# A convolution mixed with linear attention: the written-out order, the engines of the read-outs and the PSUM rings replaced by new tables

## The chip, the cores and the metric

The kernel runs on one core of a Trainium2 chip. Its engines work side by side, each through its own list of instructions in order: TensorE (PE in the profile; its weight loads are PEld), VectorE (DVE), ScalarE (ACT), GpSimd (POOL) and SyncE (SP), which issues most of the DMAs. An engine waits for another one through semaphores. The metric is the device time of one execution in microseconds; lower is better. The profile's span runs from the first to the last instruction of the program, a little less than the execution.

## The reference

Two branches share one input `x` of 2048 rows and 512 channels. Branch a is a long convolution along the rows, with one kernel for each channel that is a sum of 128 complex exponentials (written as an FFT in the reference). Branch b is a linear attention with 32 heads of 16, whose features are softmax pairs of a small learned projection. A sigmoid gate mixes them row by row.

```python
x = A_u
g = _sigmoid((x * gate_w).sum(-1, keepdims=True))
# a: K[d,l] = Re sum_n C[d,n] * exp(l*dt[d]*A[d,n]) * dt[d]*B[d,n];  y = irfft(rfft(u)*rfft(K))[:L] + u*Dskip
P = jnp.exp(logdA[:, :, None] * l[None, None, :])
K = jnp.einsum("dn,dnl,dn->dl", Cc, P, dB).real
# b: per head
phi_q = jnp.concatenate([_softmax(pq, axis=-1), _softmax(-pq, axis=-1)], axis=-1)
phi_k = jnp.concatenate([_softmax(pk, axis=-1), _softmax(-pk, axis=-1)], axis=-1)
num = jnp.einsum("bhqf,bhfd->bhqd", phi_q, kv)
den = jnp.einsum("bhqf,bhf->bhq", phi_q, z)[..., None] + 1e-6
b = (num / den) @ wo
return g * a + (1 - g) * b
```

## The kernel before

The program is a list of about a thousand steps, built by `Plan.add` and `Plan.dma`, each with its engine, its inputs and the rings of buffers that it takes and frees. `Plan.run` doesn't search for an order. It reads three tables of digits: `ORDER` names the steps in the order in which their instructions are written out, `SIDES` says of every step that may run on either of two engines which one it gets (0 or 1 of its pair; mostly copies out of PSUM, the read-outs, on ScalarE or VectorE), and `RINGS` says which of two PSUM rings a step takes its banks from. Each engine then executes its own instructions in that order. So the place of a step in `ORDER` fixes what stands ahead of it on its engine, on SyncE's queue of DMAs too.

The work falls into four stretches.

First come the loads, sine tables for the transforms (`tgs`), transposes of `x` (`xps`) and the parameters of the exponentials.

Then come the keys of the attention in eight blocks. For each block TensorE makes two `pk` tiles, ScalarE takes Exp of plus and minus each (`ek`, tile Ek, L68), VectorE sums them to Zk (`zk`), ScalarE takes Ln of Zk and Exp of minus that (`rz`: the rows Zk<-Zk and vr<-Zk), and VectorE scales the values (`vr`). Between the blocks lie the transform of `x` (`XAu`, and `XU`, which reads the tile xst out) and the tables Ctab and Dtab of the convolution's kernel, whose sines and cosines ScalarE computes (`p_sn`, tile trg).

The third and longest stretch makes the convolution's kernel in sixteen units. For a unit ScalarE takes two sines (`cs<-args`) and one Exp (`E<-args`), VectorE makes the factors A (`A1`, L1132) and R (`Rh`, `Rl`), and TensorE multiplies them with 128 small matmuls (`kps`, L178). There is one buffer for A, so the next unit's `A1` waits for this unit's `kps`. Two units make a tile that goes through the transform (`psA`, `XA`, `psB`, `XK`), the product with the transform of `x` (`t`), the way back (`psz`, `Zr`, `psy`) and out. Beside it run the queries of the attention in four blocks (`eq`, tile Eq; `z1` to `z5`, tiles zs, den and apm: Ln and Exp again).

The last stretch finishes the last units and the output.

ScalarE evaluates Exp and Ln with one table of functions and Sin with another. Both are steps of `ORDER` like any other, five of each. No dependency ties a step that uses Exp to the table that is loaded when its turn comes; only the place in `ORDER` does. Where a function is called that the loaded table lacks, the build of the program puts a table load ahead of it, under the line of the call (L68). Copies, casts and Abs (L419) work with either table.

Of the kernel before, what the change touches and what calls it, by code (L numbers as in the profile page):

```python
# [70 lines left out]
class Plan:  # L71

    DIGITS = "0123456789abcdefghijklmnopqrstuvwxyzABCDEFGHIJKLMNOPQRSTUVWXYZ-_"
    ORDER = ("0H0I0J0M0K0W000L11122x0405060B0C0D2R0P0_100Q0d0e0f0X0N0S0y0z0A0s0t0u0U0708090V13140g0h0i0j0k0l2T2y0T0Y1716192S0O0102032U"
             "2V2W0Z1a0R1y0-2X1b2Z0m0n0o0a0b0c0p0q0r0v0w0x150E0F0G2_302-1c1n181w1z312Y1H1o2B1e1f1p1g1d1A32332C2D1x351I1J342L2E2J1C2K1B"
             "1q1r1s1E2F1K2H2M362G2P1F2N3738392I2Q2O3b3a4C1t1u1v4J4K4L4M4Y4Z4-4_3c4N1Y4Q4R4O3d3f4P3g4U4S4V50514W535758544T524X5b1P591D"
             "1M551O5d5c5e3h3e5i5m5j5f5g5n565a3i3j3k5h5o5k3l5q1h1i1j5s5r5t5x3n3m5B3o1Q5u5v1R5C5l5y5w5z5p3p3r5D5F5H5G5I5M5A3s5E5U3R2z3S"
             "3q3t3u3v5W5V5N2v2w1Z1G5J1L5X5K4D5L5_1S604E5O5Q5R5Y5Z5-5S61631T3w3y1N5P3x5T3z62671U693T4F3D6465684G6a3F1V666m3U6o3G6b6n6p"
             "1W3E3A3B3C6c3K3M6q3L3N3O3P3Q6d6r3V3W6s1X1-3X6e3Y3Z3H3I3J6f3_6g3-6h2040271_41422129222b23282d241k1l1m4344456t464748494b2a"
             "2f4a4c2c254d4e4f2e2g2h262o4g2j4i4j2i4n2k4h4k4l4m2l2q2s2p6i4o2r2m4p4q4r4s4t2t4u4w4v2n2u6u4x8l4y4z4A6j6k6x8p8k4B6l6v6w8m6y"  # L80
             "6z8o8q2A6A6B8n8r6G8s4H8t6F8w8u6I6J4I8x8z8y7M7N8Q8R8v8A6H8C6K6M8W8D8S8B6N8F7O9e9f9g6L7d8E9b9c9d8I6O8G7P7e8J7f8Z8H7Q6P7g8K"
             "8-6Q8X6R6S8L9h9i9j6T7h7i8T938U8_an8M8V7jao948Nae8O7k8P6U6V6W6X6Y6Z6_70717R8Yaf90ap7l7m9192a4a8956C6D6Ea9ag6-a69673a5abah"
             "75a7akaaac747Sadai7n977o99alaj7298atam9a7p7q7r7s7t767u7v7w7y7z7AaBaCaq77au7Tar799n7U9oaHas9v9p787V7Wav9w9x7aaw9qaE9raK7X"
             "7YaL7Z9y9z7-7_809DaDaM9EaI9L9M9A9B9CaxaFayc5c6bX7x7Caz7EaGb_aA9k9l9mc09FaJ7DbY7B7G7I7FaQ9N7bc1818283858687aNaR7JbZ7HaOaP"
             "aS84899s9t9ucba_b0b1aYaZa-c7c8c2888a9GaTb-9HaU7c8b8d8fc9c3aVaW8ccPcQcRceca7K8gaXcc8e8hc4cf7Lcg9I9J9K9O8ib88j9P9Q9R9Scdcs"
             "ckchb9bgba9T9U9VcictbhclcjdYd-cBbicudZcmbocycvd_e0cCbwcnb2b3b4bpcDbxcwe1cocqczcrcxbbbje2bce3cpb5b6b7cHe4bqeUeVe59W9X9Ybd"
             "bebfcAcIbkcEdOeL9ZeMeWcFdP9-dSdTcGbye6e7e8cJblbmbna0cScTcU9_a1cKeOeRa2cLcYcZc-e9eaebdUedeeefbrcMeNa3bscNcOePbzbAc_d7eSdR"
             "e-eQecd0bBbCbDeTd1d8dfbtbubvdWcVcWcXdgegeXd2ehbEbFbGd3d9dnd4d5d6eidodQeYdae_dVeZdbdhbHbIbJfpf0dpfsftdXfqfvfrdcdddedidjbK"
             "dqbLezeAeBf1drfKbMfLf2f3dkdldmf4fwf5bNfubOfMfxfQfyf6f7fzdsdtdufNbPfAfOfReFeGeHdBfPf8bQfBfCejekfDfbfSdvdwdxdydzdAdCdEfTfc"
             "fUfVdDeCeDeEfddFf9eIeJeKfWfXfYdGdHfZfaf-fef_fffEg0elbRbSbTfFfgfGfHembUbVbWepeqerdIdJdKesg1endLdMdNeoewexeyfhg2fifmfnfofj"  # L90
             "fkfleteuevfIg3g4g5g6fJg7gbgcgdg8g9ga")
    SIDES = ("111101000110111000001000111100100110111000001100100000000001000111101010110100001000000100000001000000000000000100000000"
             "01000000000000000111000110000100000001000001100100010")
    RINGS = ("100111001111001000100000000000000000000001100000000000000001100010000000100100010000011111110110111101000010000011101010"
             "0110")
    WARM = ("000000000000000000000000000000000000000000000000000000000000000000000000000000000000000000000000000000000000000000000000"
            "000000000000000000000")
    ZPS = ("01000111")
# [49 lines left out]
    def run(self):  # L148
        code = {d: i for i, d in enumerate(self.DIGITS)}
        order = [64 * code[a] + code[b] for a, b in zip(self.ORDER[0::2], self.ORDER[1::2])] or list(range(len(self.nodes)))  # L150
        assert sorted(order) == list(range(len(self.nodes)))
        sides, rings, warm = iter(self.SIDES), iter(self.RINGS), iter(self.WARM)
        for n in self.nodes:
# [1496 lines left out]
```

## Time and profile before

| | |
|---|---|
| time, median of 3 runs | 267.77 us (266.85 to 270.31) |
| the profiled execution | 266.68 us, span 264.9 us |
| mean granted TensorE clock | 0.939 |
| VectorE busy | 225.0 us (85% of the span) |
| ScalarE busy | 220.3 us (83%) |
| TensorE matmuls busy | 198.5 us (75%), 4642 matmuls and as many weight loads |
| bytes moved by DMA | 34.63 MB |

VectorE and ScalarE are busy almost alike, and for most of the time both at once, so that neither has much room alone. TensorE's busy time is that of short, pipelined matmuls. In a row of a group of instructions the number behind x is a count, then come the busy time in us, the mean of one in ns, and the idle time of the engine just before such instructions with what ended it; "issue" stands for idle time in which the profile shows nothing that the engine waited for.

### The profile page before, as it was taken

To read this page: it belongs to the slowest core of one execution; us is meant where nothing else is said; L and a number is where in the kernel's file an instruction comes from. 1 tells how busy PE (TensorE), PEld (TensorE's weight loads), DVE (VectorE), ACT (ScalarE), POOL (GpSimd) and SP (SyncE) were. 2 spreads that over 40 slices of the span, in tenths; PEclk is the share of its full clock that TensorE was granted. 3 is DMA by queue.
4 is the path that set the end of the run, shared out by engine and by line. 5 is a ranking of instruction groups with operands and counts; after the bars stand their busy time and mean duration, and the time that the engine had idled before them with its cause. 6 is when DMAs were issued, how large, how long until landed. Compare 5 with 4: busy or idle time off the path is not lost.

```text
span 264.9 us, 10337 instructions
## 1 busy us (share of the span) xinstructions
PE 198.5 (75%) x4642; PEld 134.3 (51%) x4642; DVE 225.0 (85%) x297; ACT 220.3 (83%) x305; POOL 20.6 (8%) x36
## 2 busy tenths in 40 slices
PE   0478999999955653999566867479968888986980
PEld 0377565566634321344434635357637565875540
DVE  7698989998899999899679998667998998965771
ACT  6896878999999783999899999679998999852550
POOL 4770000000000000000000000000000000020331
PEclk9999999999997575799988999999999999999996
DMA  7899300043270743700530358921596789897316
GB/s 197 147 208 190 76 2 4 2 121 108 90 194 12 235 123 109 227 28 4 155 109 2 109 127 217 301 50 23 117 245 153 211 207 233 218 224 246 62 37 105
DMA packets 54252, 34.63 MB, mean 131 GB/s; under 512 B 34400, under 2 KB 49920, under 8 KB 53824
## 3 DMA queue, kind: packets, MB, share of 16 engines
q1 hardware_dynamic: 53664, 32.73, 49.0%
q0 software_dynamic: 544, 1.25, 2.2%
q8 instruction: 36, 0.59, 1.0%
q14 instruction: 8, 0.07, 0.1%
HBM read 21.38 MB, written 12.58 MB: 128 GB/s over the span
## 4 chain that ended last, share of the span: by engine, by line
PE 38%; ACT 31%; DVE 16%; issue 7%; SPq 3%; DMA 3%; ACTq 0%; POOLq 0%; POOL 0%; DVEq 0%
PE pk L738 5%; ACT cs L68 5%; ACT Eq L68 4%; PE vp L786 4%; PE kps L178 3%; PE psy L853 3%; PE psz L1284 3%; ACT E L68 3%; ACT XA L144 3%; DVE Ctab L393 2%; DVE Dtab L393 2%; ACT XK L144 2%; DMA XUX<-XUd 2%; ACT L65 2%; ACT Zr L144 2%
## 5 line engine op out<-in xcount | busy, mean ns | idle before, releaser
L68 ACT ACTIVATE cs<-args 128x1024 bf16<-128x1024 f32 x32 | 31.0, 1046 | 6.2 <-PE args L1055 6.2
L1132 DVE TENSOR_TENSOR A<-Ctab,Dtab 128x3072 bf16<-128x3072 bf16 x16 | 28.1, 1756 | 9.5 <-PE kps L178 9.4
L178 PE MATMUL kps<-R,A 128*32 128x64 bf16 x2048 | 21.6, 198 | 11.9 <-issue 7.8
L178 PEld LDWEIGHTS <-A 128*32 128x32 bf16 x2048 | 19.8, 116 | 15.5 <-issue 13.2
L1399 POOL DMA_DIRECT2D out_dram<-xT x10 | 6.5, 652 | 229.3 <-ACT Ctab L144 217.1
L1141 DVE TENSOR_TENSOR R<-E,cs 128x2048 bf16<-128x2048 bf16 x16 | 19.5, 1218 | 0.5 <-ACT E L68 0.5
L1145 DVE TENSOR_TENSOR R<-E,cs 128x2048 bf16<-128x2048 bf16 x16 | 19.5, 1218 | 0.1
L144 ACT CAST XA<-psA 128x1024 bf16<-128x1024 f32 (+1 forms) x15 | 14.5, 983 | 5.2 <-PE psA L185 5.1
L1256 DVE TENSOR_TENSOR t<-XUX,XK 128x2048 bf16<-128x2048 bf16 x14 | 17.0, 1219 | 2.0 <-DMA XUX<-XUd 1.2
L1284 PE MATMUL psz<-t,TI 128*128 128x512 bf16 x64 | 16.8, 380 | 2.3 <-issue 0.8
L144 ACT CAST XK<-psB 128x1024 bf16<-128x1024 f32 (+1 forms) x16 | 15.9, 1023 | 3.0 <-PE psB L191 2.5
L68 ACT ACTIVATE E<-args 128x1024 bf16<-128x1024 f32 x16 | 17.0, 1061 | 0.9 <-PE args L1077 0.9
L786 PE MATMUL vp<-WW,xT 128*128 128x512 bf16 x64 | 17.6, 410 | 0.0
L68 ACT ACTIVATE Ek<-pk 128x512 bf16<-128x512 f32 x32 | 16.5, 606 | 1.2 <-PE pk L738 1.2
L872 PE MATMUL pq<-xT,Wqp 128*128 128x512 bf16 x64 | 16.9, 401 | 0.4 <-ACT Eq L68 0.4
L68 ACT ACTIVATE Eq<-pq 128x512 bf16<-128x512 f32 (+1 forms) x28 | 16.8, 726 | 0.3 <-PE pq L872 0.3
L144 ACT CAST Zr<-psz 128x1024 bf16<-128x1024 f32 (+1 forms) x15 | 14.7, 986 | 2.5 <-PE psz L1284 2.3
L645 PE MATMUL psB<-XAu,TB 64*128 64x128 bf16 x256 | 10.7, 240 | 7.4 <-ACT xst L144 6.2
L738 PE MATMUL pk<-WW,xT 128*128 128x512 bf16 x64 | 15.0, 380 | 0.0
L645 PEld LDWEIGHTS <-TB 64*128 64x128 bf16 x256 | 8.9, 105 | 10.3 <-issue 10.2
L185 PE MATMUL psA<-W,KD 128*64 128x128 bf16 x256 | 10.0, 221 | 4.6 <-ACT XK L144 1.4
L1055 PE MATMUL args<-selE,statC 64*128 64x512 bf16 x32 | 7.8, 463 | 7.2 <-DVE xst L146 3.7
(215 smaller groups left out, 511.5 us busy)
## 6 DMA issues: line engine op xcount, KB each, us to landing
XUX<-XUd SPq DMA_DIRECT2D x32, 256.0 KB, 4.7
XUd<-xst SPq DMA_DIRECT2D x8, 512.0 KB, 3.0
ax<-apd SPq DMA_DIRECT2D x16, 256.0 KB, 4.3
Zd<-Zr SPq DMA_DIRECT2D x12, 256.0 KB, 3.9
ZT<-Zd SPq DMA_DIRECT2D x12, 256.0 KB, 5.3
UD<-in_A_u_dram SPq DMA_DIRECT2D x16, 128.0 KB, 4.3
XUd<-xst SPq DMA_DIRECT2D x8, 256.0 KB, 4.0
Dtab<-in_B_wqkv_dram SPq DMA_DIRECT2D x1, 1024.0 KB, 5.8
```

The source lines that it names most:

```text
L68: return self.nc.scalar.activation(**kw)
L144: self.nc.scalar.copy(out=o, in_=i)
L178: nc.tensor.matmul(kps[32 * dj:32 * dj + 32, g4, e, :], lhsT=A[:, d // 4, 32 * ka:32 * ka + 32, d % 4], rhs=R[:, kr, d, :], start=(i == 0) ...
L645: nc.tensor.matmul(box.ps[:, c2, sl, :], lhsT=fc.TB[rows, b0:b0 + 2].rearrange("p a b -> p (a b)"), rhs=X.t[rows, k, r0 + sl].rearrange("p ...
L738: nc.tensor.matmul(box.ps[:], lhsT=xT[:, st, kt, :], rhs=g.WW[:, kt, :], start=(kt == 0), stop=(kt == 3))
L786: nc.tensor.matmul(box.ps[:], lhsT=xT[:, st, kt, :], rhs=g.WW[:, 4 + kt, :], start=(kt == 0), stop=(kt == 3))
L872: nc.tensor.matmul(box.ps[:, m - m0, :] if late else box.ps[:], lhsT=g.Wqp[:, kt, 128 * m:128 * m + 128], rhs=xT[:, 4 * b:4 * b + 4, kt, : ...
L1132: nc.vector.tensor_tensor(out=c.A[:].rearrange("p q (o a b) l -> p (q o) a b l", o=3, a=4), in0=cf.unsqueeze(2).to_broadcast([128, 96, 8, ...
L1141: nc.vector.tensor_tensor(out=c.R[:, :, :, 32:64], in0=t.E[:, 1].unsqueeze(1).to_broadcast([128, 2, 32, 32]), in1=t.cs[:], op=ALU.mult)
L1145: nc.vector.tensor_tensor(out=c.R[:, :, :, 0:32], in0=t.E[:, 0].unsqueeze(1).to_broadcast([128, 2, 32, 32]), in1=t.cs[:, ::-1, :, ::-1], o ...
L1256: nc.vector.tensor_tensor(out=box.t, in0=Ls[r0 // ns].X[:], in1=box.XK[:].unsqueeze(1).to_broadcast([128, 2, 1024]), op=ALU.mult)
L1284: nc.tensor.matmul(box.pz[:, hb, :], lhsT=fc.TIp[:, k].rearrange("p h a t -> p (h a t)"), rhs=box.t[:, k, 512 * hb:512 * hb + 512], start= ...
```

## The change

Three tables get new values: `ORDER`, `SIDES` and `RINGS`. The steps, their instructions, their shapes and the numbers of buffers stay as they are; `WARM` and `ZPS` are not touched. Two lines of the diff stand for all:

```diff
-    ORDER = ("0H0I0J0M0K0W000L11122x0405060B0C0D2R0P0_100Q0d0e0f0X0N0S0y0z0A0s0t0u0U0708090V13140g0h0i0j0k0l2T2y0T0Y1716192S0O0102032U"
...
+    ORDER = ("070B0H0I0y0C0d000K0J0L0g0M0D0S0p0W0z150j0U110q0_2R010N0a040V0A0e0P142x2S0Q2T192U0X100r0T0m0h050O2y2V0s0R0k0n0Y2X0Z170l0-"
...
-    SIDES = ("111101000110111000001000111100100110111000001100100000000001000111101010110100001000000100000001000000000000000100000000"
...
+    SIDES = ("111101010111110100000000011101101000000000000100000000000000110101001010111110101100100100011100000000000100000000100010"
```

In `SIDES`, 23 steps go from ScalarE to VectorE and 20 the other way, six of them `XU` (tile xst). In `RINGS` 39 of the steps that may use either of two rings take the other one.

On ScalarE, among the blocks of the keys, before (Dtab is made by Exp; vb and xst are read-outs):

```order
L68 ACTIVATE Ek<-pk 128x512 x4
L144 CAST XAu<-psA 128x256x4
L68 ACTIVATE Dtab<-pt_223 128x128x4 x2
L144 CAST vb<-vp 128x512
L68 ACTIVATE Zk<-Zk 128x128
L68 ACTIVATE vr<-Zk 128x4x32
L68 ACTIVATE Ek<-pk 128x512 x4
L144 CAST xst<-psB 128x2x4x4x32
```

and at the same stage now (trg is a sine):

```order
L65 ACT_TABLE_LOAD
L144 CAST XAu<-psA 128x256x4
L68 ACTIVATE trg<-pb_220 128x1024
L68 ACTIVATE trg<-pb_219 128x1024
L144 CAST vb<-vp 128x512
L68 ACT_TABLE_LOAD
L68 ACTIVATE Zk<-Zk 128x128
L68 ACT_TABLE_LOAD
L68 ACTIVATE vr<-Zk 128x4x32
L144 CAST xst<-psB 128x2x4x4x32
L68 ACTIVATE Ek<-pk 128x512 x4
```

Before, all eight blocks' Ek, Zk and vr stand ahead of the change to the sine table; now that change (`tabT`, the row L65) stands after the second block's Ek, the sines trg stand between the later blocks, and each return from a sine to Ln and Exp has table loads under L68.

On ScalarE, at the second query block, before (cs is a pair of sines; zs and den are Ln and Exp):

```order
L68 ACTIVATE zs<-zs 128x256
L68 ACTIVATE den<-zs 128x256
L65 ACT_TABLE_LOAD
L68 ACTIVATE cs<-args 128x1024 x2
L144 CAST KD<-kps 128x1024
L68 ACTIVATE cs<-args 128x1024 x6
L144 CAST wo<-ops 128x512
L65 ACT_TABLE_LOAD
```

and now:

```order
L65 ACT_TABLE_LOAD
L68 ACTIVATE cs<-args 128x1024 x2
L68 ACT_TABLE_LOAD
L68 ACTIVATE zs<-zs 128x256
L68 ACT_TABLE_LOAD
L68 ACTIVATE den<-zs 128x256
L68 ACTIVATE Eq<-pq 128x4x128 x2
L68 ACTIVATE E<-args 128x1024
L68 ACTIVATE Eq<-pq 128x4x128 x2
L68 ACT_TABLE_LOAD
L68 ACTIVATE den<-den,eps 128x128
L68 ACT_TABLE_LOAD
```

The eight sines of four units stood together between two loads; now Ln and Exp stand between them, with a load at each turn. Over the whole program ScalarE's list has 11 rows ACT_TABLE_LOAD before (one L233, ten L65) and 53 now (one L233, ten L65, 42 L68). Of the 42, 25 stand between the early L65 load shown above and the last Eq of the first query block, and 17 between that and the last pair of sines; none stands after it. One of the ten L65 loads now stands at the end of ScalarE's list, with nothing behind it.

On VectorE, around the change from Ctab0 to Ctab1 (the eighth to the ninth A, which waits for the eighth unit's `kps`), before:

```order
L1132 TENSOR_TENSOR A<-Ctab_74,Dtab 128x3072
L1145 TENSOR_TENSOR R<-E,cs 128x64x32
L943 TENSOR_TENSOR Eq<-Eq,ax 128x2048
L1141 TENSOR_TENSOR R<-E,cs 128x64x32
L1085 TENSOR_TENSOR E<-E,Gtab 128x1024
L1132 TENSOR_TENSOR A<-Ctab_75,Dtab 128x3072
```

and now:

```order
L1132 TENSOR_TENSOR A<-Ctab_74,Dtab 128x3072
L146 CAST xT<-bps 128x4x128
L1141 TENSOR_TENSOR R<-E,cs 128x64x32
L943 TENSOR_TENSOR Eq<-Eq,ax 128x2048
L146 CAST Dtab<-ops 128x512
L943 TENSOR_TENSOR Eq<-Eq,ax 128x2048
L1085 TENSOR_TENSOR E<-E,Gtab 128x1024
L146 CAST Dtab<-ops 128x512
L1145 TENSOR_TENSOR R<-E,cs 128x64x32
L1132 TENSOR_TENSOR A<-Ctab_75,Dtab 128x3072
```

Four other steps stood between the two A; now there are eight.

More of the change, by code (lines that the diff above doesn't have):

```diff
@@ L73 @@
     DIGITS = "0123456789abcdefghijklmnopqrstuvwxyzABCDEFGHIJKLMNOPQRSTUVWXYZ-_"
-    ORDER = ("0H0I0J0M0K0W000L11122x0405060B0C0D2R0P0_100Q0d0e0f0X0N0S0y0z0A0s0t0u0U0708090V13140g0h0i0j0k0l2T2y0T0Y1716192S0O0102032U"
[L75 to L91, printed above, removed]
@@ L92 @@
-    SIDES = ("111101000110111000001000111100100110111000001100100000000001000111101010110100001000000100000001000000000000000100000000"
-             "01000000000000000111000110000100000001000001100100010")
-    RINGS = ("100111001111001000100000000000000000000001100000000000000001100010000000100100010000011111110110111101000010000011101010"
-             "0110")
+    ORDER = ("070B0H0I0y0C0d000K0J0L0g0M0D0S0p0W0z150j0U110q0_2R010N0a040V0A0e0P142x2S0Q2T192U0X100r0T0m0h050O2y2V0s0R0k0n0Y2X0Z170l0-"
+             "0v1216022H060i2Y0w1d1a0f1b08130o2I0b1y2W1c1n0E0c1o1p2Z2_1e2-2F1H031I181f1w1z30310x0t1A331J352G1S360u091x1K1g321R2B1P2v1Y"
+             "1C2C1B371q2L1r342D1E2E2J1M2P1Z2M0F1h1F2N1L382K0G2Q393b1N1s2O4C4J4L1O3c3a3d4Y1Q3f1D4K1G4M1T4N3e4Z1U3h4Q3i4O1V1W3g4-3j4_3k"
+             "3l4P1X4R4U503n4V4W3m531i4S3o3p1_1-1j3r4T3R5154521t214X3q573s5b5c5d2758593w1k5i3y555e3t2856201u5f5j5a235m3z3u5g2a3x293S5q"
+             "5n4D5s5h3A4E3v1l5r2d3D3T3B5t2z5k3F5o5l3C3G5u223E1m5v3K5x3U3L3M5y2b5p5w3V3N2e243O3X5F5z2c5H3P3W3Z3H5G5I3-5B3I3Y3_5C2g5J5A"
+             "4F5M5D5K2540412f5E3Q2i43425Q445L453J5N465R2o472h5U5O5V5W482w5_492k4b1v5S5X604a2j5Y4c4d4g5Z2A5P4e4i2q5T5-4j63262l6467654f"
+             "696e4h612m2s2n62662p4n684p4k4l6a4q2r4m6f6m6b4o4u6n4w4x6c4v4r6i6d6o2t4y6j6g4s2u6t6p8n4t6k8k6x4z6y6h6q8r6u4A4B8t8o4G6r8u8C"
+             "8D8w8x8m6G6s6I8q6K8v8y8z6v6z8l6l4H6L6H8E8A6w6A4I6B6M6J8Q8R6N6F8B9e7d8p6O8S8F8s7M6P8G8I8J7f6Q7N8H9f8K7h9h9i8Z7e6R8W7g6S8L"
+             "7O8-6C8M8X6T8N7ian8T6U6V93ao7j8O6W7k8U8Pa48_7Q6D94a87la97mae7n9j8V6X7Paf7S8Y9091ap6Y6_927Ta5ak6Z7o9b6-95aa7096a6717397ah"
+             "6E7paiagab98a7aj759c9g99alac7q749aamat72auaB777r7R9daqaCar7s79ad9naDas7t9o9p7U9v7V7a7Wav9w9xaH7uaK7876aw7y9k7z9qaLaE7A7X"
+             "7v9r7Y9y9D7w9z9s9l7xaIaQ9A9E7Z7-9L9Max7C9mc5aybXc6aM9taF7B9F9Bazb_7baGaRb27Dc07EaA7_bY809Nc1aJ7FbZ81aYaN82859Ca_aO86837G"
+             "7I7caPaSc27HaTcb84b0aZ9GaU9H9u7J8789aV888ace9Ic7cf8b9O8daW9P8c8f7Ka-ccaXb88g8ec8cscgckb9clct7Lc99J8hb18i8jb-bgdY9Kcabhba"
+             "c39QcdchcydZbo9Rbicucicjbpd-bbcmd_cze0cvbccncw9SeUe1cBbwcCcPbxcx9TcDcob5eVb3cQcqcHcpe2cIb6bjb7cAcEcFcrbkc49WdOb4cGbqe3bd"
+             "9UbldSe4dT9Xbm9Z9YcJ9Ve5cKbyeObecSeLdPe6dUcYe79-a0cTeP9_cZa1bfe8cLcReMcMcNa2c-cObrbseQeRcUc_d0bneNe9eabzeSa3edbAd1d7eeeb"
+             "btbBd8bue-ezeAdfeffpbCdgbveTd9fqd2dneXeWe_cVcWeYd3bDdodaecdbd4dRcXeZegdQeBdhfrdWdpfKfLf0dcbEf1ehfsddd5d6ftbKeidedidVfvfw"
+             "dqdjbFejdrf2bGbHbIbJfuf4f3f5bLfxbMeCdkdlbNfQeDeEekfNfObOfMf6fPdsdtfRfyfzduf7dBbPf8dmfAeIfbfcfSfTdvfdfBeJdwdyeFbUeGdxdzeH"
+             "dAdCfUdEbQeKdDfVdFfCf9dGfDdHfEfafeelffdIfgbRfWfFfXdJemfGfYenfHfZeoepeqdLf_erbVg1f-esg0dKdMg3bWfhbSetdNfig2fIg4bTg5fJeuew"
+             "dXfjg6fkfmfnflg7gbgcfoexeyg8evg9gdga")
@@ L96 @@
+    SIDES = ("111101010111110100000000011101101000000000000100000000000000110101001010111110101100100100011100000000000100000000100010"
+             "11000000000000000011000000000100010001000000000011010")
+    RINGS = ("101000011101011100100000000000000000000000000000000000000001101001000000000000010111111001111011111010101101001001001111"
+             "0011")
     WARM = ("000000000000000000000000000000000000000000000000000000000000000000000000000000000000000000000000000000000000000000000000"
```

## The prediction

> **What bounds the kernel now.** I read the page's busy times and its chain first, then the windows of the four stretches that the words on the kernel tell of, then the waits and the timeline at the places where the new lists differ.
>
> ```profile
> PE 198.5 (75%) x4642; PEld 134.3 (51%) x4642; DVE 225.0 (85%) x297; ACT 220.3 (83%) x305; POOL 20.6 (8%) x36
> PE 38%; ACT 31%; DVE 16%; issue 7%; SPq 3%; DMA 3%; ACTq 0%; POOLq 0%; POOL 0%; DVEq 0%
> ```
>
> Three engines are used to three quarters and more, and the chain passes from one to the next. No single engine is the bound over the span; which one has least room differs by stretch:
>
> ```profile
> core 0: us, PE busy (x) PEld busy (x) DVE busy (x) ACT busy (x) POOL busy (x), PEclk, DMA share, GB/s
> 0.00:45.70 45.70, 32.35 (x371) 23.79 (x372) 39.40 (x78) 37.20 (x57) 12.99 (x24) 1.00 0.59 120
> 45.70:116.60 70.90, 54.77 (x1019) 31.96 (x1018) 66.41 (x98) 62.59 (x93) 0.00 (x0) 0.83 0.40 116
> 116.60:222.00 105.40, 79.67 (x2485) 54.82 (x2485) 90.68 (x92) 98.70 (x131) 0.00 (x0) 0.98 0.53 136
> 222.00:264.90 42.90, 31.70 (x793) 23.75 (x780) 28.53 (x32) 21.78 (x29) 7.57 (x12) 0.94 0.63 153
> ```
>
> I call these A (loads, tables), B (key blocks, up to the last Eq of the first query block), C (to the last pair of sines) and D (the rest). Each row gives the length, then the busy time of each engine. The idle time that ScalarE has left is 8.5 us in A, 8.3 in B, 6.7 in C and 21.1 in D. So whatever is added to ScalarE in B and C beyond 15.0 us must make these stretches longer. TensorE leaves 16.1 and 25.7 us there.
>
> **The change: table loads.** The order shows the largest piece: ScalarE's list has 53 table loads in place of 11. Their price and places before:
>
> ```profile
> L65 ACT ACT_TABLE_LOAD  x10: 1283/1283/1283, 2.2 to 223.0; - x10
> L233 ACT ACT_TABLE_LOAD x1 | 1.3, 1283 | 0.7 <-PEq L1634 0.7
> 0.00:45.70 45.70, 2.57 (x2) 1.00 0.59 120
> 45.70:116.60 70.90, 2.57 (x2) 0.83 0.40 116
> 116.60:222.00 105.40, 6.42 (x5) 0.98 0.53 136
> 222.00:264.90 42.90, 1.28 (x1) 0.94 0.63 153
> ```
>
> The first row gives the shortest, the median and the longest of ten loads, in ns: all alike. The four window rows count the loads of L65 by stretch. L233's lies in A, so before there are 3, 2, 5 and 1. By the new order there are 3, 26, 23 and 1, and the one in D stands last on ScalarE, where nobody waits for it. That is 24 more in B (24 x 1.283 = 30.8 us) and 18 more in C (23.1 us), 53.9 us in all.
>
> A load stands in ScalarE's own list, so what follows waits. It could cost more than its duration (a pause around it) or less (it runs while ScalarE waits for an operand). The timeline of ScalarE around one of them, and at two functions that follow each other without one (start, duration):
>
> ```profile
> 13.52 1.04 ACT L68 ACTIVATE TB<-tgv 128x1024 bf16<-128x1024 f32 x1
> 14.58 1.28 ACT L65 ACT_TABLE_LOAD   x1
> 15.87 0.63 ACT L68 ACTIVATE pt<-ld 128x512 f32<-128x512 bf16 x1
> 16.41 0.19 ACT L68 ACTIVATE dtc<-ldc 128x4 f32<-128x4 bf16 x1
> ...
> 70.38 0.31 ACT L68 ACTIVATE Zk<-Zk 128x128 f32<-128x128 f32 x1
> 70.73 0.31 ACT L68 ACTIVATE vr<-Zk 128x128 bf16<-128x128 f32 x1
> ```
>
> TB ends at 14.56, the load starts 0.02 later and ends at 15.86, and the next function starts 0.01 after it: no pause on either side. The two functions behind overlap by 0.09 (15.87 + 0.63 = 16.50 against 16.41). A load put between two that overlap costs this overlap too: 0.09 + 0.03 = 0.12 us each. Zk and vr, a Ln and an Exp of its result, don't overlap (70.69 against 70.73), so the loads inside such a pair (nine of the 42: seven in B, two in C) lose nothing. That leaves 18 x 0.12 = 2.2 us in B and 15 x 0.12 = 1.8 in C.
>
> The Trainium skill (ScalarE: Activation LUTs, What ACT_TABLE_LOAD costs) speaks harder against the change: a switch to another set is about 1283 ns of load and about 1380 ns of drain, 2.66 us together. The trace agrees with the first figure and shows nothing of the second (0.02 us ahead of the load at 14.58). By the page alone my estimate would be 58 us more.
>
> How much hides in idle time? ScalarE's two largest waits in B and C:
>
> ```profile
> ACT cs L68 <- PE args L1055: 5.1, 3, 4.2
> PE args L1055 <- DVE xst L146: 3.7, 1, 3.7
> ACT Dtab L144 <- PE ops L962: 2.6, 1, 2.6
> ```
>
> The first (us in all, times, longest) is in B: cs waits for args, and args for a read-out xst that stands late on VectorE. All six xst that VectorE has go to ScalarE now, so this cause goes. What remains of the idle is 3.2 us beyond it in B and 6.7 in C. With ScalarE loaded by a third more, what it waits for will mostly be done in time. The ends are 0 (all filled) and 8.3 and 6.7 (nothing filled). I take 2.0 in each, nearer to the lower end, as an engine that has become the sole bound mostly finds its operands ready, but VectorE's sums between Ek and Zk still have to be waited for.
>
> **Read-outs on other engines.** 23 steps leave ScalarE and 20 come to it.
>
> ```profile
> L144 ACT CAST xst<-psB 128x1024 bf16<-128x1024 f32 x10 | 9.8, 1009 | 0.2 <-ACT pmag L68 0.2
> L146 DVE CAST xst<-psB 128x1024 bf16<-128x1024 f32 x6 | 7.2, 1213 | 0.0
> ```
>
> The six xst add 6 x 1.009 = 6.1 us to ScalarE and take 7.3 off VectorE; the other steps go mostly the other way and nearly level that. Three steps fewer at about 1 us bound the net on ScalarE by -3 and, with shorter ones leaving than coming, +3. I take 0. VectorE has 4.5 us of room in B and 14.7 in C before the change, and tens of us once ScalarE stretches both, so 3 us more or less there are covered by ScalarE.
>
> **TensorE's order and supply.** TensorE's instructions come in blocks, 36 of them and 0.59 MB (16 KB each):
>
> ```profile
> q8 instruction: 36, 0.59, 1.0%
> PEld L178 <- issue: 13.2, 15, 2.7
> PE kps L178 <- issue: 7.8, 5, 2.6
> DVE A L1132 <- PE kps L178: 9.4, 7, 3.2
> 173.01 1.76 DVE L1132 TENSOR_TENSOR A<-Ctab,Dtab 128x3072 bf16<-128x3072 bf16 x1 [3.24 <-PE kps L178]
> 170.03 2.57 issue
> ```
>
> Weight loads and matmuls of `kps` stall without any releaser, up to 2.7 us at a time, and VectorE's A waits 9.4 us for `kps` in all. The row at 173.01 is the ninth A, which waits 3.24 us; the last row is the chain's step ahead of it. Four more steps now stand between the eighth and ninth A on VectorE, so this wait should go. The gain has the ends 0 and 9.4 us. While ScalarE bounds B and C it is worth nothing there, since VectorE would wait for cs and E instead. I count 0 in B and C. In D:
>
> ```profile
> 220.89 1.15 ACT L68 ACTIVATE cs<-args 128x1024 bf16<-128x1024 f32 x1
> 222.96 1.28 ACT L65 ACT_TABLE_LOAD   x1
> 224.26 1.02 ACT L68 ACTIVATE E<-args 128x1024 bf16<-128x1024 f32 x1
> 225.31 1.23 DVE L1141 TENSOR_TENSOR R<-E,cs 128x2048 bf16<-128x2048 bf16 x1
> 245.50 1.07 ACT L144 CAST XA<-psA 128x512 bf16<-128x512 f32 x2 [5.14 <-PE psA L185]
> ```
>
> The last sine ends at 222.04; then come a load and an Exp, and R starts only at 225.31. In the new list no load and no Exp that R needs stands behind the last sines, so R follows them at once: -3.3 us. The 5.14 us that XA waits for psA near the end stay; it is D's own end of the range below.
>
> **Rings and loads.** 39 steps take another PSUM ring. A step that finds its ring full waits for a read-out, which in B and C waits for ScalarE anyway; cost 0, with the idle terms above as ends. On SyncE's queue the early loads stand in another order, the one of wqkv still second:
>
> ```profile
> PE wtp L559 <- DMA Dtab<-in_B_wqkv_dram: 7.1, 1, 7.1
> UD<-in_A_u_dram SPq DMA_DIRECT2D x16, 128.0 KB, 4.3
> ```
>
> Stretch A cannot be shorter than VectorE's 39.4 us (-6.3). One transfer more ahead of the awaited one is about +4.3. I take 0.
>
> **The sum**, in us: A 45.7. B 62.6 + 30.8 + 2.2 + 2.0 = 97.6. C 98.7 + 23.1 + 1.8 + 2.0 = 125.6. D 42.9 - 3.3 = 39.6. The span is 308.5. The profiled execution took 266.68 us, 1.8 more than its span of 264.9, so the time is 310.3, which I round to 310. The median of the runs (267.77) is 1.1 above the profiled execution; that stays inside the range.
>
> **The rivals.**
>
> First, not slower: the loads hide. Place: ScalarE's waits in B and C, 15.0 us; price: what a load costs beyond them. All of that idle and all of VectorE's 9.4 us for `kps` against whole loads give 266.7 + 53.9 - 15.0 - 9.4 = 296.2, still 11% more. To end under +2% (272.0 on the profiled execution) a load may cost (272.0 - 266.7 + 24.4) / 42 = 0.71 us on the path; at 0.6 us the time would be 267. For it: a load needs no operand, so it can run while ScalarE waits. Against it: all ten rows read 1283 ns.
>
> Second, nothing is absorbed: the idle stays, since ScalarE, VectorE and TensorE wait for each other in turn. Then 264.9 + 53.9 + 1.8 = 320.6. For it: 31% of the chain is ScalarE and 38% TensorE, so waits alternate. Against it: the cause of the longest wait, xst on VectorE, moves.
>
> Third, the new order is good in all else: no idle in B and C (93.4 and 121.8 us) and the 5.14 us wait in D gone (34.5): 45.7 + 93.4 + 121.8 + 34.5 + 1.8 = 297.2. For it: TensorE's stalls grow less when its work is spread over a longer time. Against it: the pairs of Ln and Exp wait for VectorE's sums.
>
> Fourth, each load also stops ScalarE for as long again, with its pipeline emptied first: 310.3 + 53.9 = 364. The gap of 0.02 us ahead of the load speaks against it. This is the rule of the Trainium skill named above (ScalarE: Activation LUTs, What ACT_TABLE_LOAD costs), whose own figure would give about 368.
>
> **How the numbers follow.** The forecast with its neighbours (303 to 316) has 0.66, nothing absorbed 0.15, all else good 0.12, not slower 0.03, a second stop at each load 0.02; 0.02 is left for what I don't see. The range goes from 296, which takes in the third rival, to 321, the second; with A's ends, the overlap and the idle terms inside it. Under 2% is about what a measurement of this kernel cannot tell from no change: faster has 0.01, within 2% 0.02 and slower 0.97, since four of the five cases lie at 297 and above, and the not-slower one lies mostly within.
>
> **What would show it.** In the profile after: 42 rows ACT_TABLE_LOAD under L68 at 1283 ns and ScalarE's busy time near 274 us, 88% of the span or more. B near 98 us, C near 126, D near 40. VectorE's idle time grows and is ended by ScalarE's cs, E, Ek, while its wait for `kps` at the ninth A is gone. Loads that start with no gap behind the function before them show the fourth rival wrong. I am wrong if ScalarE's busy time rises by the 54 us while the span rises by less than 30, or if B or C shows 5 us or more of idle time on ScalarE.

## The result, and the profile after

The changed kernel takes 307.02 us (median of 4 runs, 305.48 to 307.59) against 269.04 us for the kernel before beside it (266.85 to 271.90). The ratio is 1.143, with a 95% interval of 1.133 to 1.154. Ratios here and below are of fast executions only: the few that took over 1.5% more than the fastest of their kernel, as the 271.90 us here, are left out of them. The forecast was 310.

The profiled execution took 307.59 us, its span 305.8. The page's busy times of the changed kernel (busy us, share of the span, instructions):

```profile
PE 210.0 (69%) x4621; PEld 140.9 (46%) x4642; DVE 226.3 (74%) x300; ACT 274.2 (90%) x344; POOL 20.9 (7%) x36
```

ScalarE went from 83% to 90% and from 220.3 to 274.2 us. VectorE did the same work (226.3 us), but its share fell from 85% to 74%. The increase is 53.9 us on one engine, and the groups of ScalarE's instructions name it (busy us, mean ns, idle time ahead; then shortest, median and longest):

```profile
L68 ACT ACT_TABLE_LOAD x42 | 53.9, 1283 | 0.8
L65 ACT ACT_TABLE_LOAD x10 | 12.8, 1283 | 0.2
...
L68 ACT ACT_TABLE_LOAD  x42: 1283/1283/1283, 43.3 to 264.7; - x42
```

The 42 loads cost 1283 ns each, as did the ten before. The stretches are cut at the end of the first query block's last Eq, the eighth, at 138.9, and at the end of the last sine, at 268.0. (The prediction's cut at 116.6 falls into the seventh Eq; the eighth ended at 117.5.) The first border of the prediction has no counterpart, because the key blocks and the sines now interleave across it, so A and B are taken together. First the changed kernel:

```profile
core 0: us, PE busy (x) PEld busy (x) DVE busy (x) ACT busy (x) POOL busy (x), PEclk, DMA share, GB/s
0.00:138.90 138.90, 90.75 (x1351) 56.29 (x1367) 99.83 (x172) 133.41 (x174) 13.38 (x24) 0.88 0.39 94
138.90:268.00 129.10, 90.75 (x2578) 62.82 (x2574) 101.77 (x103) 122.75 (x146) 0.00 (x0) 0.91 0.50 130
268.00:305.80 37.80, 28.54 (x716) 21.82 (x717) 24.66 (x26) 18.02 (x26) 7.56 (x12) 0.92 0.56 127
```

and the kernel before over A and B:

```profile
0.00:116.60 116.60, 87.12 (x1388) 55.74 (x1389) 105.81 (x176) 99.79 (x148) 12.99 (x24) 0.90 0.47 118
```

A and B grew from 116.6 to 138.9 us, C from 105.4 to 129.1 (from 117.5 and 104.5, if both are cut at the end of the eighth Eq), and D shrank from 42.9 to 37.8. ScalarE idles 5.5 us in A and B (16.8 before) and 6.4 in C (6.7 before): it is the bound of both.

How one key block looks now, on ScalarE's timeline of the changed kernel (start, duration), and the one instruction of VectorE's timeline that waits for it:

```profile
81.86 1.06 ACT L68 ACTIVATE trg<-pb 128x1024 bf16<-128x1024 int16 x1
82.83 1.91 ACT L144 CAST XAu<-psA 128x1024 bf16<-128x1024 f32 x2
84.75 1.28 ACT L68 ACT_TABLE_LOAD   x1
86.05 0.31 ACT L68 ACTIVATE Zk<-Zk 128x128 f32<-128x128 f32 x1
86.38 1.28 ACT L68 ACT_TABLE_LOAD   x1
87.67 0.31 ACT L68 ACTIVATE vr<-Zk 128x128 bf16<-128x128 f32 x1
```

```profile
88.01 0.69 DVE L795 TENSOR_TENSOR vr<-vb,vr 128x1024 bf16<-128x1024 bf16 x1 [3.46 <-ACT vr L68]
```

Two loads of 1.28 us stand around a Ln of 0.31, and VectorE waits 3.46 us for the result. What is late next, from the waits of the changed kernel (us in all, times, longest):

```profile
DVE vr L795 <- ACT vr L68: 15.7, 6, 5.1
DVE E L1085 <- ACT E L68: 8.3, 4, 3.3
DVE vr L795 <- ACT vb L144: 6.8, 2, 4.1
ACT KD L144 <- PE kps L178: 6.5, 2, 3.7
DVE A L1132 <- PE kps L178: 4.7, 5, 1.6
DVE R L1141 <- ACT cs L68: 4.4, 2, 3.2
```

VectorE's largest waits are now for ScalarE: for vr, the result behind two loads, for E and for the read-out vb. Its wait for `kps` at A halved, from 9.4 to 4.7 us.

### The profile page after: what moved, and what is told of

Read it like the earlier page. It is cut to its first block, busy times and chain, and to the rows that moved or that the text cites. A ratio compares the mean times of both kernels' runs of the same rounds, so it can differ in the third digit from the quotient of the medians.

```text
span 305.8 us, 10348 instructions
## 1 busy us (share of the span) xinstructions
PE 210.0 (69%) x4621; PEld 140.9 (46%) x4642; DVE 226.3 (74%) x300; ACT 274.2 (90%) x344; POOL 20.9 (7%) x36
## 5 line engine op out<-in xcount | busy, mean ns | idle before, releaser
L68 ACT ACT_TABLE_LOAD x42 | 53.9, 1283 | 0.8
L68 ACT ACTIVATE cs<-args 128x1024 bf16<-128x1024 f32 x32 | 31.0, 1026 | 0.1
L178 PE MATMUL kps<-R,A 128*32 128x64 bf16 x2048 | 22.5, 204 | 11.0 <-issue 5.6
L178 PEld LDWEIGHTS <-A 128*32 128x32 bf16 x2048 | 20.8, 118 | 15.9 <-issue 13.7
L795 DVE TENSOR_TENSOR vr<-vb,vr 128x1024 bf16<-128x1024 bf16 x16 | 10.6, 688 | 22.6 <-ACT vr L68 15.7
L68 ACT ACTIVATE Ek<-pk 128x512 bf16<-128x512 f32 x32 | 17.0, 611 | 0.7 <-PE pk L738 0.6
L738 PE MATMUL pk<-WW,xT 128*128 128x512 bf16 x58 | 17.3, 433 | 0.5 <-issue 0.2
L1085 DVE TENSOR_TENSOR E<-E,Gtab 128x1024 bf16<-128x1024 bf16 x16 | 11.0, 686 | 8.3 <-ACT E L68 8.3
L68 ACT ACTIVATE Eq<-pq 128x512 bf16<-128x512 f32 (+1 forms) x28 | 16.9, 690 | 0.0
L144 ACT CAST Zr<-psz 128x1024 bf16<-128x1024 f32 (+1 forms) x14 | 13.9, 1008 | 3.1 <-PE psz L1284 3.1
L68 ACT ACTIVATE E<-args 128x1024 bf16<-128x1024 f32 x16 | 16.6, 1049 | 0.0
L620 PE MATMUL psA<-W,UDp 128*128 128x256 bf16 x64 | 11.3, 309 | 7.3 <-ACT XAu L144 3.8
L185 PE MATMUL psA<-W,KD 128*64 128x128 bf16 x256 | 11.3, 242 | 6.8 <-ACT E L68 5.6
```

Source lines behind the costliest of these rows:

```text
L68: return self.nc.scalar.activation(**kw)
L144: self.nc.scalar.copy(out=o, in_=i)
L178: nc.tensor.matmul(kps[32 * dj:32 * dj + 32, g4, e, :], lhsT=A[:, d // 4, 32 * ka:32 * ka + 32, d % 4], rhs=R[:, kr, d, :], start=(i == 0) ...
L185: nc.tensor.matmul(ps[64 * ri:64 * ri + 64], lhsT=lhsT, rhs=fc.W1[:, ri].rearrange("p r d -> p (r d)"), start=True, stop=True, tile_positi ...
L738: nc.tensor.matmul(box.ps[:], lhsT=xT[:, st, kt, :], rhs=g.WW[:, kt, :], start=(kt == 0), stop=(kt == 3))
```

## The experiments

Three questions: are the table loads the whole loss, what is the rest of the change worth without them, and can the loads be had few and that worth be kept? Lines are numbered a little higher in the kernels whose table helper is longer.

### e1, e2: the loads taken away, in the new order and in the old

The same edit on both kernels. It replaces part of the computation, so the results are no longer those of the reference: the sines of trg and cs become exponentials, and the changes to the sine table ahead of them load the table of Exp and Ln.

```diff
-        S("p_sn", lambda: act(out=F.sc[:, 0], in_=X(), func=ACT.Sin, scale=TURN), r="act B0", w="s0")
+        S("p_sn", lambda: act(out=F.sc[:, 0], in_=X(), func=ACT.Exp, scale=TURN), r="act B0", w="s0")
...
-            act(out=T.cs[:, 0], in_=i, func=ACT.Sin, scale=TWO_PI_S, bias=QUARTER_PI)
+            act(out=T.cs[:, 0], in_=i, func=ACT.Exp, scale=TWO_PI_S, bias=QUARTER_PI)
...
-    trg = P.add("ACT", "tabT", lambda: act.begin(TRIG), rw=("", "act"), sets="T")
+    trg = P.add("ACT", "tabT", lambda: act.begin(LN_EXP), rw=("", "act"), sets="T")
...
```

> The changed kernel, but the sines of trg and cs are computed as Exp, and the changes to the sine table ahead of them load the table of Exp and Ln instead (the output's sines are replaced by exponentials; the sines of the first tables stay). 42 of the 53 table loads fall away, 11 stay, as many as before. Theory (the 42 loads are the whole loss, the order itself is no worse): between 253 (307.0 less 53.9) and 268. Rival (the loads are only part; the new order keeps VectorE and TensorE waiting by itself): 275 to 295.

> The kernel before with the same replacement (sines of trg and cs as Exp; 11 loads as it has). It shows what the replacement does by itself. Both theories: 266 to 271, since a sine and an Exp of this shape take 1.05 and 1.06 us and no load is added or taken away. The first run is read against this one: the difference is what the order, the engines of the read-outs and the rings are worth without the loads. Theory: the first run is up to 4% below this one; rival: it is 3% or more above.

Measured: 256.34 us (ratio to the kernel before 0.951, interval 0.947 to 0.955) and 269.90 us (1.003, interval 0.999 to 1.006). The control does not move, so the edit itself is free in the old order. Without its 42 loads the new kernel is 5.0% faster than the control (256.34 against 269.90), not slower, and by more than the 4% expected; the loads account for the whole loss and more: 307.0 - 256.3 = 50.7 us, or 1.21 us each. The rival, an order that is bad by itself, falls.

Where the 5% lies: busy times and the wait at A, first of e1, then of e2:

```profile
PE 196.9 (77%) x4642; PEld 134.5 (53%) x4642; DVE 224.5 (88%) x300; ACT 218.2 (86%) x302; POOL 20.9 (8%) x36
...
PEld L178 <- issue: 14.3, 16, 2.5
DVE A L1132 <- PE kps L178: 4.0, 4, 1.4
```

```profile
PE 200.6 (75%) x4642; PEld 136.4 (51%) x4642; DVE 225.0 (84%) x297; ACT 220.3 (82%) x305; POOL 20.5 (8%) x36
...
PEld L178 <- issue: 11.2, 15, 1.7
DVE A L1132 <- PE kps L178: 10.6, 7, 3.3
```

The engines do nearly the same work in 13.3 us less span (254.5 against 267.8). VectorE's wait at A for `kps` is 4.0 in place of 10.6 us. The stalls of the weight loads for `kps` without a releaser did not get fewer (14.3 against 11.2): the new order does not remove them. It has other work stand where VectorE would have waited at A, and a part of the wait only moved: VectorE waits 2.3 us for `ops` at the read-out Dtab (0.7 in e2) and 7.0 for `psy` at the output (3.0 in e2). So this is a part of the 13.3 us and not all of it. TensorE's granted clock was also higher, 0.961 in e1 against 0.912 in e2, and its busy time 3.7 us less; what that is worth was not tried.

### e3: the new order, a load only at need

```diff
     def begin(self, name):
-        return self.nc.scalar.preload_act_table_set(name)
+        return None

     def __call__(self, **kw):
+        want = {ACT.Sin: TRIG, ACT.Exp: LN_EXP, ACT.Ln: LN_EXP}.get(kw.get("func"), self.cur)
+        if want != self.cur:
+            self.nc.scalar.preload_act_table_set(want)
+            self.cur = want
         return self.nc.scalar.activation(**kw)
```

> The changed kernel with its own order and results, but tables are loaded only at need: the steps tabT and tabL load nothing, and ahead of a Sin, or of a Ln or Exp, the one table that serves it is loaded where another is in place. 36 loads in place of 53. Theory (each load costs its 1.283 us): 17 x 1.283 = 21.8 less, 285 (281 to 290). Rival (loads lie mostly in time when ScalarE would have waited): 297 or more.

Measured: 290.0 us (ratio 1.073, interval 1.066 to 1.081), at the upper end of what was expected. ScalarE in this run:

```profile
PE 206.4 (72%) x4642; PEld 137.7 (48%) x4642; DVE 225.0 (78%) x300; ACT 251.7 (88%) x327; POOL 21.2 (7%) x36
...
L70 ACT ACT_TABLE_LOAD x35 | 44.9, 1283 | 0.6
```

By the spans of the profiled executions (305.8 for the changed kernel, 287.1 here, 254.5 in e1), 17 loads fewer saved 18.7 us, 1.10 each; the 25 that still stand above e1's 11 cost 32.6, 1.30 each. Nine of the 17 were the second load of a Ln and Exp pair. No step was moved for it.

### e4: 42 loads in the old order

```diff
+    EXTRA = {34 + 66 * k // 24 for k in range(24)} | {100 + 4 * k for k in range(18)}
...
     def __call__(self, **kw):
+        self.due += self.calls in self.EXTRA
+        self.calls += 1
+        if self.due and not self.fresh:
+            self.nc.scalar.preload_act_table_set(self.cur)
+            self.due -= 1
+        self.fresh = False
         return self.nc.scalar.activation(**kw)
```

> The kernel before with 42 more loads of the table that is in place anyway: 24 spread evenly over the functions of the stretch of the key blocks, 18 over those up to the last sines, the counts of the changed kernel there. Results and order stay. Theory (a load costs its duration less the idle time that it fills, at most 15.0 us in these two stretches): 268 + 53.9 - 15.0 = 307 to 322. Rival (the loads themselves are mostly hidden, and the changed kernel loses by its order): 270 to 295.

Measured: 316.85 us (ratio 1.176, interval 1.172 to 1.180), 47.5 us above the kernel before, 1.13 per load. The page's busy times:

```profile
PE 216.6 (69%) x4642; PEld 143.8 (46%) x4642; DVE 227.5 (72%) x297; ACT 277.8 (88%) x347; POOL 20.7 (7%) x36
```

So loads alone, with no other change, give a loss of that size: 47.5 us for 42 of them here, 50.7 in the new order. The span splits into ScalarE's busy and idle time; idle is span less busy:

| | span | ScalarE busy | ScalarE idle |
|---|---|---|---|
| before | 264.9 | 220.3 | 44.6 |
| after | 305.8 | 274.2 | 31.6 |
| e1 (after, 11 loads) | 254.5 | 218.2 | 36.3 |
| e3 (after, 36 loads) | 287.1 | 251.7 | 35.4 |
| e4 (before, 53 loads) | 315.0 | 277.8 | 37.2 |

From e1 to after, 42 loads add 56.0 us of busy time and fill 4.7 of idle time; from before to e4 they add 57.5 and fill 7.4. Of the changed kernel's 31.6 us of idle time 19.8 lie in D (37.8 - 18.02), where no load stands that anything waits for: idle time far from a load cannot take it in.

### e5, e6: order and sides apart

```diff
-    SIDES = ("111101010111110100000000011101101000000000000100000000000000110101001010111110101100100100011100000000000100000000100010"
+    SIDES = ("111101000110111000001000111100100110111000001100100000000001000111101010110100001000000100000001000000000000000100000000"
...
```

This is e5's edit (it takes the old `RINGS` too, in the form of e1); e6 is the reverse, the new `SIDES` in the kernel before.

> The new ORDER alone, with the SIDES and RINGS of before, in the form of the first run (sines of trg and cs as Exp, 11 loads). It splits the 5% by which that run lies under its control (256.3 against 269.9). Theory (the order carries the gain, since the wait of A for kps fell from 9.4 to 4.0 us with A's place on VectorE): 255 to 262. Rival (the read-outs' engines and the rings carry it): 266 or more.

> The kernel before with the new SIDES alone: 23 read-outs from ScalarE to VectorE, 20 the other way; order, rings, sines and the 11 loads stay. Theory (the new sides fit the new order and are worth nothing in the old one): 267 to 275. Rival (the sides carry the gain): 258 to 264.

Measured: 285.91 us and 289.67 us (ratios 1.062, interval 1.053 to 1.071, and 1.077, interval 1.068 to 1.085). Both theories were wrong on this. e5 lies where its rival had it (266 or more), but the rival's cause, that the sides and rings carry the gain, is not borne out: in e6 the new sides lose too. The new sides together with the new rings in the old order were not run. Neither part that was run alone carries the gain: the new order with the old sides and rings is 29.6 us slower than with its own, and the old order with the new sides about 20 slower than with its own. The waits, first of e5, then of e6:

```profile
DVE A L1132 <- PE kps L178: 15.2, 5, 4.8
ACT KD L144 <- PE kps L178: 8.9, 6, 4.7
ACT Zk L68 <- DVE Zk L765: 7.6, 2, 6.8
```

```profile
ACT zs L68 <- PE zs L896: 7.4, 1, 7.4
DVE Zk L768 <- PE zk L759: 7.1, 3, 4.1
```

The Zk of 6.8 us can be followed on VectorE's timeline of e5:

```profile
60.90 1.21 DVE L146 CAST xst<-psB 128x1024 bf16<-128x1024 f32 x1
62.42 1.21 DVE L146 CAST xst<-psB 128x1024 bf16<-128x1024 f32 x1
63.55 2.33 DVE L765 TENSOR_REDUCE Zk<-Ek 128x64 f32<-128x1024 bf16 x2
```

The sides of before put these read-outs xst on VectorE, ahead of the sum Zk that ScalarE's Ln waits for; in e1 ScalarE makes the xst of this stage itself, and its Ln does not wait. So a read-out on the other engine stands in the way of other work there. In e5 A also waits 15.2 us for `kps` in place of e1's 4.0; what makes those `kps` late was not followed. Whether sides or rings do more of it in e5 was not tried.

### e7 to e11: orders with few loads

All five load at need as e3 does and take a new `ORDER` made from a coarse account of the steps' durations. The longest run of steps that kept their sequence has 311 to 370 of the 1038. e7 and e8 start from the new kernel, e9 from the old one; e10 (from the old) and e11 (from the new) also put 46 and 51 read-outs on the other engine. Of e10:

```diff
-    ORDER = ("0H0I0J0M0K0W000L11122x0405060B0C0D2R0P0_ ...
+    ORDER = ("0H0I0J000M0L11120g0h0B0C0D0y04052R0z0s0j ...
...
```

> All results as the reference's. Tables are loaded only at need, SIDES and RINGS are the new ones, and ORDER is the new one with steps moved so that sines stand together again: 19 loads in place of 53. Theory (a load costs 1.1 to 1.35 us, as the runs so far show, and the rest of the new order is worth 5%): 256.3 + 8 x 1.2 = 266, less what the moves win, 254 to 266, below the kernel before. Rival (moving the sines gives up what the new order had won): 268 or more.

> As the run before it, with another set of moves and also 19 loads. Theory: 254 to 266; rival: 268 or more. Where the two differ by more than 3 us, the count of loads is not what sets the time at this level.

> All results as the reference's. The kernel before with its SIDES and RINGS, tables loaded only at need, and ORDER moved step by step from the old one, 15 loads in place of 11. It asks whether the old order has slack that moves alone can win at nearly the old count of loads. Theory (the loads are the loss, and an order with few of them keeps a gain): 256 to 266. Rival (an order is worth what its fine timing is worth on the chip, and moves made by a coarse account of durations lose it, as the two regrouped ones did): 270 or more.

> As the run before it, with 46 read-outs on the other engine besides, set together with the moves; 15 loads. Theory (order and sides fitted together win, as 256.3 against 269.9 showed, and either alone loses 6 to 8%): 252 to 264, below the run before it. Rival: 270 or more.

> The new ORDER and SIDES moved together in the same manner, tables loaded only at need, 19 loads. Theory: 256.3 + 8 x 1.2 = 266 or less, 254 to 266. Rival: 270 or more, as the first two regrouped orders (276.6 and 285.5).

| | loads | us | ratio to before, 95% interval |
|---|---|---|---|
| e7 | 19 | 276.61 | 1.032 (1.022 to 1.042) |
| e8 | 19 | 285.51 | 1.057 (1.045 to 1.069) |
| e9 | 15 | 273.87 | 1.017 (1.008 to 1.026) |
| e10 | 15 | 265.87 | 0.987 (0.979 to 0.995) |
| e11 | 19 | 271.93 | 1.007 (1.001 to 1.013) |

e7, e8, e9 and e11 went the rival's way. e7 and e8 have the same 19 loads and differ by 8.9 us, so at this level the count of loads does not set the time; e8 is as slow as e5 with 11. Because the steps were shuffled so widely, these runs do not price the loads in the new order. e10 is the only one of the five below the kernel before, by 1.3% (0.5 to 2.1% by its interval), which is less than the 2% that counts as a clear difference here. It lies below e9, as the theory had it, and just above its 252 to 264. Its busy times, loads and the wait at A:

```profile
PE 198.7 (75%) x4642; PEld 134.0 (51%) x4642; DVE 234.2 (89%) x305; ACT 219.2 (83%) x301; POOL 20.9 (8%) x36
...
L70 ACT ACT_TABLE_LOAD x14 | 18.0, 1283 | 0.2
...
DVE A L1136 <- PE kps L182: 1.0, 1, 1.0
```

VectorE idles 30.0 us (264.2 - 234.2), against 39.9 before, and A hardly waits, but 9 us of work more lie on VectorE. An order with e1's 256 us and the true sines was not found.

## Why the prediction was right

**The table loads** (24 more in B, 18 in C, 53.9 us): right to the digit in the profile, and e1, e2 and e4 show that they are the cause. The step that counted, reading ScalarE's list for what the build puts in, held.

**No pause around a load**: right. The load at 86.38 starts 0.02 us after Zk ended (86.05 + 0.31). The rival with a second stop (364) is refuted: 42 loads cost 1.21 us each on the path. The Trainium skill (ScalarE: Activation LUTs, What ACT_TABLE_LOAD costs) gives 2.66 us for a switch with its drain; the measurement disagrees: each load took 1.283 us, and the one at 86.38 began 0.02 us after the function ahead of it.

**Lost overlap** (+4.0) **and read-outs** (0): both off by about 2 us, in opposite directions. e1's ScalarE is busy 2.1 us less than before with as many loads, which fits its three instructions fewer (302 against 305); after is 56.0 above e1, where the loads are 53.9, so the lost overlap is about 2.1. That the two cancel, so that ScalarE's busy time rose by just the 53.9 us of the loads, is luck.

**Idle time**: the sum was near, its parts were not. A with its 8.5 us of idle time was kept and B was given 2.0; measured are 5.5 in the two together, so A and B came out at 138.9, not 143.3. C was given 2.0 and shows 6.4, so it came out at 129.1, not 125.6. (Cut at the end of the eighth Eq, each of the two differences is 0.9 us larger.) With D the three lengths are off by -4.4, +3.5 and -1.8 us; that these partly cancel, so that 310 stands beside 307, is luck. The prediction named 5 us or more of idle time on ScalarE in C as a sign of being wrong, and C shows 6.4: the loads and the time came out as forecast, but the statement that ScalarE's idle time in C would mostly fill did not hold; it fell only from 6.7 to 6.4. In C the largest single piece is this, from ScalarE's timeline and the chain of waits:

```profile
201.52 1.01 ACT L144 CAST KD<-kps 128x1024 bf16<-128x1024 f32 x1 [3.69 <-PE kps L178]
```

```profile
197.69 3.22 issue
```

KD waits for `kps`, and TensorE stalls 3.22 us there without a releaser. The statement that a bound engine mostly finds its operands ready missed that a stall of TensorE reaches ScalarE too. It is the term of C that was furthest off; ScalarE's busy time there was 122.8 us where 123.6 were counted.

**D** (-3.3, to 39.6): right in kind. The last sine ends at 267.95 and R starts at 267.99, with no load and no Exp between (ScalarE's and VectorE's timelines):

```profile
266.01 1.94 ACT L68 ACTIVATE cs<-args 128x1024 bf16<-128x1024 f32 x2
```

```profile
207.29 1.75 DVE L1132 TENSOR_TENSOR A<-Ctab,Dtab 128x3072 bf16<-128x3072 bf16 x1
...
267.99 1.23 DVE L1141 TENSOR_TENSOR R<-E,cs 128x2048 bf16<-128x2048 bf16 x1 [3.24 <-ACT cs L68]
```

D is 37.8, another 1.8 shorter. The wait of 5.14 us for psA that the prediction kept there is not found again: the longest for psA in D is now 2.29. What the 1.8 us come from was not followed further.

**TensorE's order and supply, counted 0 in B and C**: the order gave C no gain to speak of, as counted, since ScalarE bounds it (its idle time there fell from 6.7 to 6.4); but TensorE's stalls were not worth 0, as KD has shown. As a statement on the order the 0 hides much: e1 shows it is worth 13.6 us with the sides and rings that belong to it. The ninth A (the row at 207.29 above) has no wait, as foretold. But two instructions ahead of it VectorE waits, at one of the read-outs that now stand between the two A:

```profile
205.54 0.69 DVE L146 CAST Dtab<-ops 128x512 bf16<-128x512 f32 x1 [3.80 <-PE ops L962]
```

Before, VectorE waited 3.24 us at this A. So the wait moved to another row and did not go. The third rival (297) had a good order in view. Its A and B, 139.1 us together, are near what was measured (138.9), but by luck: it kept 8.5 us of idle time in A and none in B, where the two show 5.5. It fails in C (121.8 against 129.1) and D (34.5 against 37.8).

**What VectorE waits for**: cs and E were named and hold (4.4 and 8.3 us); the largest, vr with 15.7 us, was not. It is the result behind two loads.

The first rival (not slower, 267) needed a load under 0.71 us; the runs give 1.1 to 1.3. The second (nothing absorbed, 320.6) is refuted for this kernel by 13.0 us less idle time, of which e1 shows 8.3 to come from the new order, engines and rings and 4.7 from the loads.

## What to carry to other kernels

Read the instruction list that the build makes, not only the steps: an order that is free to mix functions of two tables gets a load at each turn, on the engine with the least room, and the steps' list does not show it. Price inserted work on a saturated engine at its full duration less only the idle time that lies where it stands; here 42 loads of 1.283 us cost 47 to 51 us. An order, the engines of its read-outs and its rings belong together in this kernel: against the kernel before, the new order with the old engines and rings lost 6%, the new engines with the old order and rings 8%; all three together and without the loads won 5%.

## What the runs showed that was not expected

- A Ln and an Exp of its result, with no table named ahead, got two loads, one for each (as at 84.75 and 86.38); with the set of both named ahead (e3), one served. The Trainium skill (ScalarE: Activation LUTs, Table sets: the hidden batching unit) counts one load for Ln and then Exp; the trace shows that only where the set is asked for by name.
- The gain of the new order came without fewer stalls in TensorE's supply: 14.3 us of weight-load stalls at `kps` in e1, 11.2 in its control.
- TensorE's granted clock differed from run to run: 0.961 in e1 (span 254.5 us), 0.939 before (264.9), 0.912 in e2 (267.8), 0.931 in e5 (285.7), 0.895 after (305.8), 0.861 in e4 (315.0). It was lowest in the longest runs but did not follow the span in step. Its cause was not tried, and what part of the differences in time it makes neither.
